# Attention threshold by a parametric relu on ScalarE, q and k loaded into both partition halves, score and output banks shared, whole jobs throughout

## The chip, the cores and the metric

The kernel runs on one core of one Trainium2 chip. The metric is the time of one execution on the device in microseconds (us). TensorE (PE) multiplies, VectorE (DVE) and ScalarE (ACT) work on tiles, GpSimd (POOL) works on tiles in SBUF only, and SyncE (SP) issues the DMAs. Weight loads of TensorE are listed as an engine of their own (PEld).

## The reference

Two stages: an attention that keeps only scores within tau of the row's maximum, and an RWKV channel-mixing layer (called FFN below) over the heads put side by side.

```
q, k, v: (8 batches, 8 heads, 576, 64);  w_k: 512x1024, w_v: 1024x512, w_r: 512x512
scores = 0.125 * q @ k^T                                  # 576 x 576 per head
scores = where(scores >= max(scores) - tau, scores, -1e9) # row by row, tau = 0.02
attn   = exp(scores - max(scores)) / (sum + 1e-9)
x      = (attn @ v), heads side by side                   # 8 x 576 x 512
x_prev = x shifted by one position along the sequence
xk = mu_k*x + (1-mu_k)*x_prev;  xr = mu_r*x + (1-mu_r)*x_prev
out = sigmoid(xr @ w_r) * (relu(xk @ w_k)**2 @ w_v)
```

## The kernel before

**Jobs.** Two heads of a batch make a job; four jobs make a batch, 32 jobs in all. The 576 query rows of a head go as four units of 128 rows ("P" units, both heads, eight score matmuls into two score tiles) and one unit for the last 64 rows of both heads together ("T" unit, eight matmuls, one score tile). So a job has nine softmax passes over a tile of 128x576. Batch 0 alone is cut into eight half jobs (rows 0 to 255, then the rest), so that its first FFN chunk can begin early.

**A softmax pass.** Scores lie in a pair of PSUM banks (tag `s`, two pairs). DVE takes the negated row maximum (L605); ACT makes the threshold column from it (L613) and the exponential of the scores into SBUF (L621); DVE reads scores and exponentials, zeroes what lies under the threshold and sums the rest (L629); DVE inverts the sum (L639, L640), POOL multiplies by it (L654), DVE transposes 32x32 blocks in place (L671, L675). `PV` (L705) multiplies by v: per job 288 small matmuls in one stretch with one weight load each, into four single banks (tag `w`, four banks, shared with the FFN), which ACT copies into `xT` and `xE` (L719, L726).

**Operands.** Matmuls of q and k run in a rounded format, so each is split into a rounded high part and a low rest, stacked on the two partition halves. One DMA each brings q and k; ACT scales q (L429) and rounds both (L469), POOL subtracts (L477), and twelve DMAs move the parts within SBUF to the halves where the matmul wants them (`st<-hiq` and the like). The first job does without (L543).

**FFN.** A chunk is 256 positions: ACT, DVE and POOL make the mixed inputs (L791 to L821), TensorE runs 96 matmuls of 256 columns (L843), 24 of 512 (L885) and 48 of 512 (L907), ACT, POOL and DVE finish (L851 to L913). There are 18 chunks; a batch gives two once its jobs are done, and every fourth batch a third. The 20 weight pieces are prepared in the first stretch, with four DVE passes each (L372 to L403).

**What sets the order.** The order of every engine's instructions is fixed when the program is built: `Plan` lists all steps with a cost and a key, plays them through and issues them in the order of that play. `NUDGE` shifts keys per kind of step. Engines then run their own instructions in this order and wait for each other.

Of the kernel before, what the change touches and what calls it, by code (L numbers as in the profile page):

```python
# [7 lines left out]
F32 = mybir.dt.float32  # L8
# [6 lines left out]

W_MIN = 2.0 ** (0x38 * 2 - 127)
# [24 lines left out]
class Step:  # L41
    __slots__ = (
        "eng", "occ", "lat", "fn", "key", "deps", "succ", "allocs", "idx", "missing", "ready",
        "start", "end", "kb", "soft", "att", "kind",
# [3 lines left out]
class Plan:  # L48
# [3 lines left out]
    HOP, LATE, FROM, AHEAD = 0.05, 0.2, 200.0, 1000.0  # L52
    SOFT = {"DVE": 0.15, "ACT": 0.15}
    NUDGE = {
# [7 lines left out]
    }  # L62

# [12 lines left out]
    def add(self, eng, occ, fn, reads=(), writes=(), key=0.0, lat=None, kb=0, wait=0.0, kind=None):  # L76
        s = Step()
        s.soft = self.SOFT.get(eng, 0.0) if self.soft else 0.0
        s.att = eng == "PE" and key < -500
        if s.att:  # L80
            key += 1000 - self.AHEAD
        s.eng, s.occ, s.fn, s.kb, s.kind = eng, occ, fn, kb, kind
        s.key = key + self.NUDGE.get(kind, 0.0)
# [40 lines left out]
    def order(self, loose=()):  # L124
# [23 lines left out]
        pipe = 0.0  # L148
        out = []
# [22 lines left out]
        while len(out) < total:  # L172
            best = None
            for e, cand in open_.items():
                f = free[e]
                pick = None
                for i in cand:
                    s = steps[i]
                    t = when(s)
                    if t is None:  # L180
                        continue
                    t = max(t, f)
                    k = (t + s.soft, s.key, i, t)
                    if pick is None or k < pick:
                        pick = k
# [8 lines left out]
            free[e] = t + s.occ  # L194
# [3 lines left out]
            else:  # L198
                s.end = t + s.lat
# [11 lines left out]
            for j in s.succ:  # L211
# [4 lines left out]
                n.ready = max(n.ready, t + s.occ if same else s.end + self.HOP + late)  # L216
# [13 lines left out]
def tile_threshold_attention_then_rwkv_ffn(  # L230
# [17 lines left out]
    B, NPAIR, _, _ = qk.shape  # L248
# [9 lines left out]
    W = 2 * S  # L258
# [17 lines left out]
    HALF = 1  # L276
    W0, W1, W2, W3, AVK = 0.653, 1.950, 42.500, 5.365, 1.0
    KC, MV, RES = 2, 0.031, 3
    PREP, VB, LB = 8, 1, {"q": 1, "k": 1}
# [8 lines left out]
    def fixed(name, shape, dtype=F32):  # L288
# [17 lines left out]
        lambda: V.tensor_scalar(small.get()[:, 1:2], small.get()[:, 0:1], 0.0, -1.0, op0=ALU.max, op1=ALU.mult),  # L306
        reads=[(small, 0)],
        writes=[(small, 1)],
        key=-100, kind="dve1",
# [112 lines left out]
    def operands(job, key):  # L422
        b, hp = job["b"], job["hp"]

        def scaled(t):
            add(
                "ACT",
                0.67,
                lambda: A.activation(t()[:, 0:S], t()[:, 0:S], AF.Copy, scale=small.get()[:, 2:3]),  # L429
                reads=[(small, 2)],  # L430
                writes=[raw],
                key=key - PREP, kind="act3",
            )

        if job["plain"]:
            raw = job["raw"] = sbuf("st1", [P, W], F32, 3)
            add("DMA", DQ, lambda: SY.dma_start(raw.get(), qk[b, hp]), writes=[raw], key=key - PREP - 5, kb=576, kind="dma3")
            scaled(raw.get)
# [9 lines left out]
        if job["plain"]:  # L448
            return
        hi, lo = job["hi"], job["lo"] = {}, {}  # L450
        st = job["st"] = [(sbuf("st1", [P, W], FR, 3), sbuf("st2", [P, S], FR, 3)) for _ in range(2)]
        up, dn = slice(0, D), slice(D, P)
        for x, o in (("q", 0), ("k", S)):
            raw = lo[x] = sbuf("lo" + x, [P, S], FR, LB[x])
            top = hi[x] = sbuf("hi" + x, [P, S], FR, 1)
            add(
                "DMA",
                DQ,
                lambda raw=raw, o=o: SY.dma_start(raw.get().bitcast(F32), qk[b, hp, :, o : o + S]),
                writes=[raw],  # L460
                key=key - PREP - 5,
                kb=288, kind="dma5",
            )
            if x == "q":
                scaled(lambda raw=raw: raw.get().bitcast(F32))
            add(
                "ACT",
                0.62,
                lambda raw=raw, top=top: A.activation(top.get(), raw.get().bitcast(F32), AF.Copy),  # L469
                reads=[raw],  # L470
                writes=[top],
                key=key - PREP, kind="act4",
            )
            add(
                "POOL",
                1.39,
                lambda raw=raw, top=top: G.tensor_tensor(  # L477
                    raw.get(), raw.get().bitcast(F32), top.get().bitcast(F32), op=ALU.subtract
                ),
                reads=[top],  # L480
                writes=[raw],
# [538 lines left out]
```

## Time and profile before

| | |
|---|---|
| runs timed | median 1134.08 us of 3 (1131.31 to 1139.18) |
| profiled execution | 1133.43 us, span 1131.3 us |
| PE busy | 922.5 us, 82% of the span |
| DVE busy | 841.9 us, 74% |
| ACT busy | 649.1 us, 57% |
| POOL busy | 573.1 us, 51% |
| DMA | 147.83 MB moved, 131 GB/s on average |

The span is the profile's first to last instruction; the execution's own time lies 2.1 us above it. Matmuls overlap, so a busy share of PE counts some time twice, and so do the others where an instruction starts before the last has written back.

### The profile page before, as it was taken

Reading aid. Unit: us, or ns where it says so; the run is one execution under the profiler, and the core shown is the slowest. Engines: PE = TensorE matmul, PEld = TensorE weight load, DVE = VectorE, ACT = ScalarE, POOL = GpSimd, SP = SyncE. Lnnn points to the kernel's source line nnn. Section 1 sums busy time; section 2 is a strip of 40 time slices with the busy share of each in tenths; the row PEclk is TensorE's granted clock in tenths of the full one; section 3 lists DMA queues with packets and bytes.
Section 4 is the critical chain, followed back from the end, with each engine's and each line's share of the span. In section 5 each row is a group of like instructions: output and inputs, shape, how many; then the busy total and the mean of one; then the engine's idle time right before and its main releaser. Section 6 shows DMA issues by size and latency. Waiting matters only on the chain.

```text
span 1131.3 us, 35156 instructions
## 1 busy us (share of the span) xinstructions
PE 922.5 (82%) x14672; PEld 822.8 (73%) x14672; DVE 841.9 (74%) x1657; ACT 649.1 (57%) x1492; POOL 573.1 (51%) x582
## 2 busy tenths in 40 slices
PE   2334677787688898899899889988989898999988
PEld 2324566776578887888788778877878787888877
DVE  5776977788887888798889798978887988821120
ACT  3434663565456675667576657665766675634432
POOL 3444744454445555565555555555555555443431
PEclk9655788799688999999999999999999999999989
DMA  9376657645444445454545445554545454100000
GB/s 305 110 238 181 213 142 204 175 133 145 128 127 127 141 133 145 129 146 127 139 135 146 127 130 143 131 143 117 146 133 138 128 153 116 57 20 19 20 19 19
DMA packets 57581, 147.83 MB, mean 131 GB/s; under 512 B 9680, under 2 KB 9680, under 8 KB 52816
## 3 DMA queue, kind: packets, MB, share of 16 engines
q1 hardware_dynamic: 57424, 145.60, 45.5%
q8 instruction: 116, 1.90, 0.7%
q14 instruction: 41, 0.34, 0.1%
HBM read 74.19 MB, written 9.44 MB: 74 GB/s over the span
## 4 chain that ended last, share of the span: by engine, by line
PE 49%; DVE 24%; issue 12%; ACT 9%; POOL 5%; DMA 1%; SPq 0%; POOLq 0%; ACTq 0%; DVEq 0%
PE w L705 16%; PE s L559 9%; PE w L843 9%; PE w L907 8%; DVE sq L671 6%; PE w L885 6%; DVE sm L605 6%; DVE sq L629 6%; DVE r L800 3%; ACT sq L621 3%; POOL sq L654 2%; PE s L526 1%; ACT k L856 1%; ACT sm L613 1%; DVE sg L913 1%
## 5 line engine op out<-in xcount | busy, mean ns | idle before, releaser
L654 POOL TENSOR_SCALAR sq<-sq,sm 128x576 f32<-128x576 f32 x288 | 227.3, 802 | 235.5 <-DVE sm L640 228.0
L605 DVE TENSOR_REDUCE sm<-s 128x1 f32<-128x576 f32 x288 | 212.5, 751 | 117.1 <-PE s L559 102.3
L705 PE MATMUL w<-sq,v 32*64 32x144 f32 (+2 forms) x10368 | 193.3, 297 | 121.3 <-issue 98.2
L705 PEld LDWEIGHTS w<-sq,v 32*64 32x64 f32 x10368 | 172.3, 146 | 142.3 <-issue 114.2
L629 DVE SCALAR_TENSOR_TENSOR sq<-s,sm,sq 128x576 f32<-128x576 f32 x288 | 226.2, 803 | 24.7 <-ACT sq L621 23.3
L843 PE MATMUL w<-xk,wk 128*128 128x256 f32 x1728 | 226.9, 289 | 8.1 <-ACT xk L813 4.0
L843 PEld LDWEIGHTS w<-xk,wk 128*128 128x128 f32 x1728 | 221.0, 195 | 11.3 <-POOL xk L821 5.0
L907 PE MATMUL w<-wv,k 128*128 128x512 f32 x864 | 214.8, 396 | 0.4 <-ACT xE L726 0.4
L621 ACT ACTIVATE sq<-s,sm 128x576 f32<-128x576 f32 x288 | 208.9, 726 | 0.2
L671 DVE STREAM_TRANSPOSE sq<-sq 128x1152 f32<-128x1152 f32 x128 | 175.4, 1371 | 16.1 <-POOL sq L654 15.9
L907 PEld LDWEIGHTS w<-wv,k 128*128 128x128 f32 x864 | 161.3, 191 | 31.2 <-ACT xE L726 0.7
L559 PE MATMUL s<-st 128*128 128x288 f32 x504 | 125.4, 333 | 56.9 <-DVE sq L629 41.6
L613 ACT ACTIVATE sm<-sm,small 128x1 f32<-128x1 f32 x288 | 83.8, 291 | 151.1 <-DVE sm L605 139.5
L559 PEld LDWEIGHTS s<-st 128*128 128x128 f32 x504 | 89.5, 205 | 84.0 <-issue 58.8
L821 POOL TENSOR_TENSOR xk<-r,xk 128x512 fp32r<-128x512 f32 x72 | 92.4, 1283 | 101.8 <-ACT xk L813 100.7
L866 POOL TENSOR_TENSOR k<-r,k 128x512 fp32r<-128x512 f32 x72 | 93.9, 1305 | 73.1 <-ACT k L856 73.0
L559 PE MATMUL s<-st,st 128*128 128x288 f32 x504 | 117.0, 315 | 0.6 <-issue 0.6
L800 DVE SCALAR_TENSOR_TENSOR r<-r,mu_sb,xT 128x256 f32<-128x256 f32 x128 | 74.3, 620 | 52.5 <-POOL r L791 44.1
L885 PE MATMUL w<-wr,xk 128*128 128x512 f32 x432 | 107.8, 391 | 0.0
L719 ACT ACTIVATE xT<-w 128x128 f32<-128x128 f32 (+1 forms) x144 | 34.5, 288 | 99.7 <-PE w L705 99.7
L559 PEld LDWEIGHTS s<-st,st 128*128 128x128 f32 x504 | 89.2, 207 | 1.1 <-issue 1.1
L885 PEld LDWEIGHTS w<-wr,xk 128*128 128x128 f32 x432 | 78.1, 188 | 13.2
(55 smaller groups left out, 899.1 us busy)
## 6 DMA issues: line engine op xcount, KB each, us to landing
v<-in_v SPq DMA_DIRECT2D x36, 1152.0 KB, 5.1
st<-hiq SPq DMA_DIRECT2D x140, 144.0 KB, 2.5
st<-loq SPq DMA_DIRECT2D x140, 144.0 KB, 2.6
loq<-in_qk SPq DMA_DIRECT2D x35, 288.0 KB, 2.9
lok<-in_qk SPq DMA_DIRECT2D x35, 288.0 KB, 3.0
st<-hik SPq DMA_DIRECT2D x70, 144.0 KB, 2.8
st<-lok SPq DMA_DIRECT2D x70, 144.0 KB, 3.0
out<-sg SPq DMA_DIRECT2D x32, 256.0 KB, 2.3
```

The lines of the kernel that those rows point to most:

```text
L559: PE.matmul(ss[y].get()[:, z, 0:HS], l.get()[:, c * P : (c + 1) * P], r.get()[:, keys(z)], start=(j == 0), stop=(j == 1),)
L605: lambda sv=sv, col=col: V.tensor_reduce(col(0), sv(), axis=AX.XY, op=ALU.max, negate=True),
L613: lambda col=col: A.activation(col(1), col(0), AF.Identity, bias=small.get()[:, 1:2], scale=-1.0),
L621: lambda st=st, pv=pv, col=col: A.activation(pv(), st(), AF.Exp, bias=col(0)),
L629: lambda st=st, pv=pv, col=col: V.scalar_tensor_tensor(pv(), st(), col(1), pv(), op0=ALU.is_ge, op1=ALU.mult, accum_out=col(2)),
L654: lambda y=y: G.tensor_scalar(part(y), part(y), sm.get()[:, 3, y : y + 1], 0.0, op0=ALU.mult, op1=ALU.add),
L671: V.transpose(t, t)
L705: PE.matmul(os[a].get()[hs, 0:n], vt.get()[rows, j, hs], sq.get()[rows, j, h, lo:hi], start=(j == 0), stop=(j == NB - 1),)
L800: V.scalar_tensor_tensor(d.get()[:, y, o : o + n], diff.get()[:, y, o : o + n], mu_sb.get()[:, j, hc + y : hc + y + 1], prv[:, hc + y], op ...
L843: PE.matmul(h.get()[:, f], l, r, start=(ct == 0 and i == 0), stop=(ct == NCT - 1 and i == 2))
L885: PE.matmul(z.get(), l, r, start=(ct == 0 and i == 0), stop=(ct == NCT - 1 and i == 2))
L907: PE.matmul(vps.get(), l, r, start=(ft == 0 and i == 0), stop=(ft == NFT - 1 and i == 2))
```

## The change

The mask is made on ACT. The bias column is the negated maximum plus tau; a parametric relu with slope 1e30 leaves scores above the threshold as they are (shifted by tau) and throws those below far down, straight out of PSUM into SBUF (L640); a second pass in place takes the exponential with a bias of minus tau and sums the row (L648). DVE keeps the maximum and a one-column addition (L632) in place of the mask. The host lays each head of q and k out twice, once per partition half, and a DMA per head brings each (L463, L471); ACT rounds q with its scale (L498) and k (L480), DVE makes the low part of q in one pass (L508), POOL subtracts on one half of k (L488); no move within SBUF is left. `PV` writes two pairs of tag `s`, which has three pairs now; `w` has two banks for the FFN alone. The output copies are two per kind and job (L743, L750). `PV` is issued in three pieces, the second and third not before a set distance from the one ahead. Batch 0 has whole jobs like the others, and the first job has no path of its own. `Plan` also has a term for the fetch of PE's instructions in blocks of 256, and new tables of numbers.

```diff
-    SOFT = {"DVE": 0.15, "ACT": 0.15}
+    SOFT = {"DVE": 0, "ACT": 0}
...
+    CHUNK, FETCH = 256, 3.55
...
+            if s.ni:
+                more = self.CHUNK - code % self.CHUNK
+                code += s.ni
+                while more <= s.ni:
+                    at = t + stall + s.occ * more / s.ni
+                    stall += max(0.0, turned + self.FETCH - at)
...
+        for h in range(2):
+            rk, rq = sbuf("rk", [P, S], F32, RB), sbuf("rq", [P, S], F32, RB)
...
+                lambda rk=rk, both=both: A.activation(both.get(), rk.get(), AF.Copy),
...
+                    both.get()[D:P], rk.get()[D:P], both.get()[D:P].bitcast(F32), op=ALU.subtract
...
+                lambda rq=rq, top=top, low=low: V.scalar_tensor_tensor(
...
-            for h in range(2):
-                sl = slice(h * D, (h + 1) * D)
-                moves = [(st[h][0], up, top), (st[h][0], dn, raw)]
...
-        ss = {y: psum("s", [P, 2, 512], 2) for y in ys}
+        ss = {y: psum("s", [P, 2, 512], 3) for y in ys}
...
-                lambda col=col: A.activation(col(1), col(0), AF.Identity, bias=small.get()[:, 1:2], scale=-1.0),
+                "DVE",
+                0.1,
+                lambda col=col: V.tensor_scalar(col(1), col(0), small.get()[:, 1:2], None, op0=ALU.add),
...
-                lambda st=st, pv=pv, col=col: A.activation(pv(), st(), AF.Exp, bias=col(0)),
+                lambda st=st, pv=pv, col=col: A.activation(pv(), st(), AF.Prelu, bias=col(1), alpha=STEEP),
...
-                lambda st=st, pv=pv, col=col: V.scalar_tensor_tensor(
-                    pv(), st(), col(1), pv(), op0=ALU.is_ge, op1=ALU.mult, accum_out=col(2)
...
+                lambda y=y, col=col: A.activation(part(y), part(y), AF.Exp, bias=small.get()[:, 3:4], accum_out=col(2)),
...
-        os = [psum("w", [P, 512], 4) for _ in range(4)]
+        os = [psum("s", [P, 2, 512], 3) for _ in range(2)]
...
+                after=(prev, GAP * ni) if k else None,
...
-            h = psum("w", [P, 2, CH], 4)
+            h = psum("w", [P, 2, CH], NF)
...
-    halved = {j: ([0, 1], [2, "T", 3]) for j in range(HALF)}
-    PLAIN = 1
...
-    plan.order(loose=("w", "r"))
+    plan.order(loose=("w", "r", "s", "sm"))
```

Two places show how the order moves. The first is PE in the middle of the program: before, the last three rows of a job's `PV` (`w_67..` are its output banks), the score matmuls that follow (`s_69..`) and the FFN (L843).

```order
L705 MATMUL w_6742<-sq_6218,v_6476 64x144
L705 MATMUL w_6744<-sq_6218,v_6476 64x144
L705 MATMUL w_6746<-sq_6218,v_6476 64x144
L559 MATMUL s_6906<-st_2_6554 128x288 x2
L559 MATMUL s_6906<-st_2_6554,st_1_6570 128x288 x2
L559 MATMUL s_6916<-st_1_6279 128x288 x2
L559 MATMUL s_6916<-st_1_6279,st_0_6288 128x288 x2
L843 MATMUL w_6925<-xk_6375,wk_0_585 128x256 x3
```

The same kind of place in the change: the end of the second piece of a job's `PV`, six FFN matmuls (L932, the old L907), and the start of the third piece; `s_7081` and `s_7084` are the pairs that the job's output fills.

```order
L717 MATMUL s_7084<-sq_6616,v_6844 64x144 x2
L717 MATMUL s_7081<-sq_6616,v_6844 64x144 x2
L717 MATMUL s_7084<-sq_6616,v_6844 64x144 x2
L932 MATMUL w_7146<-wv_0_1336,k_0_6656 128x512 x3
L932 MATMUL w_7146<-wv_0_1428,k_0_6656 128x512 x3
L717 MATMUL s_7081<-sq_6616,v_6844 64x144 x2
L717 MATMUL s_7084<-sq_6616,v_6844 64x144 x2
```

Before, all 144 rows of a job's `PV` stand in one stretch with nothing between; now FFN or score matmuls stand between its three pieces. After the last `PV` of the program, four FFN chunks and half of an L907 stage follow before; three chunks and a little over half of such a stage follow now.

The second place is ACT in the middle of the program, before: threshold columns (`sm`), exponentials out of the score tiles (`sq<-s`) and the FFN's relu, square and copy.

```order
L613 ACTIVATE sm_6818<-sm_6818,small 128x1
L621 ACTIVATE sq_6647<-s_6906,sm_6818 128x18x32
L613 ACTIVATE sm_6935<-sm_6935,small 128x1
L621 ACTIVATE sq_6647<-s_6916,sm_6935 128x18x32
L851 ACTIVATE r_6968<-w_6925 128x512
L852 ACTIVATE r_6968<-r_6968 128x512
```

In the change, with relus out of the score tiles (L640), exponentials in place with their sums (L648), and the rounding of q and k (L498, L480):

```order
L640 ACTIVATE sq_6207<-s_6447,sm_6388 128x18x32
L838 ACTIVATE xk_6256<-r_6491 128x512
L648 ACTIVATE sq_6207,sm_6388<-sq_6207,small 128x18x32
L498 ACTIVATE qa_6523<-rq_6142,small 128x576
L480 ACTIVATE kc_6529<-rk_6160 128x576
L640 ACTIVATE sq_6207<-s_6471,sm_6514 128x36x16
L640 ACTIVATE sq_6207<-s_6462,sm_6479 128x18x32
L648 ACTIVATE sq_6207,sm_6514<-sq_6207,small 128x36x16
```

The one-column step is gone from ACT, and each pass over a score tile stands twice, once out of PSUM and once in SBUF.

## Rows read from the trace of the kernel before

**Rows 1.** Windows: engines' busy time (instructions), clock, DMA, in three stretches.

```profile
0.00:200.00 200.00, 104.23 (x2351) 91.33 (x2352) 150.88 (x268) 95.70 (x222) 97.39 (x89) 0.75 0.67 198
200.00:998.00 798.00, 695.89 (x11563) 623.24 (x11561) 669.50 (x1330) 505.12 (x1189) 430.18 (x451) 0.96 0.48 133
998.00:1131.30 133.30, 122.43 (x760) 108.19 (x760) 21.53 (x61) 48.31 (x82) 45.55 (x43) 0.97 0.06 19
```

**Rows 2.** Windows of line L605 alone, the row maximum, one per softmax pass.

```profile
0.00:200.00 200.00, 27.08 (x37) 0.75 0.67 198
200.00:998.00 798.00, 185.41 (x252) 0.96 0.48 133
```

**Rows 3.** The chain that ended last, around one `PV` in the middle.

```profile
571.25 3.68 PE w L705 x218
574.93 0.98 issue
575.92 1.45 PE w L705 x68
```

**Rows 4.** Waits (engine, line, what for): totals over 0 to 200 us.

```profile
PEld w L705 <- issue: 56.1, 16, 9.4
```

**Rows 5.** Waits, totals over 200 to 998 us.

```profile
PEld w L705 <- issue: 56.8, 51, 2.6
...
PEld s L559 <- issue: 41.3, 43, 3.7
```

**Rows 6.** Timeline of PE: starts of score matmuls, and of what follows eight.

```profile
561.16 0.43 PE L559 MATMUL s<-st 128*128 128x288 f32 x2
...
562.23 4.11 PE L843 MATMUL w<-xk,wk 128*128 128x256 f32 x33
```

**Rows 7.** The chain that ended last, in the stretch after the last `PV`.

```profile
998.67 1.31 PE w L705 x64
...
1036.13 10.88 PE w L843 x89
1047.00 5.48 PE w L885 x24
...
1065.48 10.89 PE w L843 x89
...
1115.70 10.89 PE w L907 x48
```

**Rows 8.** Groups by line and shape: count, busy us, mean ns of one, idle before.

```profile
L629 DVE SCALAR_TENSOR_TENSOR sq<-s,sm,sq 128x576 f32<-128x576 f32 x288 | 226.2, 803 | 24.7 <-ACT sq L621 23.3
L621 ACT ACTIVATE sq<-s,sm 128x576 f32<-128x576 f32 x288 | 208.9, 726 | 0.2
...
L613 ACT ACTIVATE sm<-sm,small 128x1 f32<-128x1 f32 x288 | 83.8, 291 | 151.1 <-DVE sm L605 139.5 <-DVE sm L639 8.8
...
L429 ACT ACTIVATE loq<-loq,small 128x576 f32<-128x576 f32 x35 | 26.9, 767 | 0.0
...
L469 ACT ACTIVATE hiq<-loq 128x576 fp32r<-128x576 f32 x35 | 23.6, 675 | 0.2
...
L629 DVE DVE_READ_ACCUMULATOR sq<-s,sm,sq 128x1 f32 x288 | 23.5, 82 | 0.0
...
L386 DVE TENSOR_SCALAR xT<-xT 128x512 uint32<-128x512 uint32 x20 | 12.8, 646 | 0.1
...
L639 DVE TENSOR_SCALAR sm<-sm 128x1 f32<-128x1 f32 x32 | 4.7, 146 | 0.5
```

**Rows 9.** Timeline of ACT: an exponential and the next instruction's start.

```profile
563.28 0.72 ACT L621 ACTIVATE sq<-s,sm 128x576 f32<-128x576 f32 x1
563.91 0.28 ACT L613 ACTIVATE sm<-sm,small 128x1 f32<-128x1 f32 x1
```

**Rows 10.** Timeline: scores of one tile begin on PE, and its mask on DVE.

```profile
549.00 0.67 PE L559 MATMUL s<-st 128*128 128x288 f32 x2
...
552.61 0.82 DVE L629 SCALAR_TENSOR_TENSOR sq<-s,sm,sq 128x576 f32<-128x576 f32 x1
```

More of the change, by code (lines that the diff above doesn't have):

```diff
@@ L14 @@
 U32 = mybir.dt.uint32
+STEEP = 1e30
+TAU = 110.0
 W_MIN = 2.0 ** (0x38 * 2 - 127)
@@ L198, in order @@
             else:
-                s.end = t + s.lat
+                s.end = t + s.lat + stall
             for b in s.allocs:
@@ L215, in order @@
                 late = self.LATE if n.att and t > self.FROM else 0.0
-                n.ready = max(n.ready, t + s.occ if same else s.end + self.HOP + late)
+                n.ready = max(n.ready, t + s.occ + stall if same else s.end + self.HOP + late)
                 if n.missing == 0:
@@ L423, in operands @@
         b, hp = job["b"], job["hp"]
-        def scaled(t):
+        job["st"] = []
+        for h in range(2):
+            rk, rq = sbuf("rk", [P, S], F32, RB), sbuf("rq", [P, S], F32, RB)
+            add(
+                "DMA",
+                DQ,
+                lambda rq=rq, h=h: SY.dma_start(rq.get(), qk[b, hp, h, :, :S]),
+                writes=[rq],
+                key=key - PREP - 5,
+                kb=288, kind="dma5",
+            )
+            add(
+                "DMA",
+                DQ,
+                lambda rk=rk, h=h: SY.dma_start(rk.get(), qk[b, hp, h, :, S:]),
+                writes=[rk],
+                key=key - PREP - 5,
+                kb=288, kind="dma3",
+            )
+            top, low, both = (sbuf(t, [P, S], FR, 3) for t in ("qa", "qb", "kc"))
@@ L432, in scaled @@
+            add(
+                "ACT",
+                0.7,
+                lambda rq=rq, top=top: A.activation(
+                    top.get(), rq.get(), AF.Copy, scale=small.get()[:, 2:3]
+                ),
+                reads=[rq, (small, 2)],
+                writes=[top],
                 key=key - PREP, kind="act3",
             )
[L435 to L438, printed above, removed]
+            add(
+                "DVE",
+                0.8,
+                lambda rq=rq, top=top, low=low: V.scalar_tensor_tensor(
+                    low.get(),
+                    rq.get(),
+                    small.get()[:, 2:3],
+                    top.get().bitcast(F32),
+                    op0=ALU.mult,
+                    op1=ALU.subtract,
+                ),
+                reads=[rq, top, (small, 2)],
+                writes=[low],
+                key=key - PREP, kind="dve7b",
+            )
@@ L439, in operands @@
+            job["st"].append((top, low, both))
         vt = job["v"] = sbuf("v", [P, NB, P], F32, VB)
@@ L447, in operands @@
         )
[L448 to L481, printed above, removed]
-                key=key - PREP, kind="pool2",
-            )
-            for h in range(2):
-                sl = slice(h * D, (h + 1) * D)
-                moves = [(st[h][0], up, top), (st[h][0], dn, raw)]
-                if x == "q":
-                    moves += [(st[h][1], dn, top), (st[h][1], up, raw)]
-                for dst, rows, src in moves:
-                    fn = (lambda dst=dst, rows=rows, src=src, sl=sl, o=o: SY.dma_start(
-                        dst.get()[rows, o : o + S].bitcast(F32), src.get()[sl].bitcast(F32)
-                    ))
-                    add("DMA", DQ, fn, reads=[src], writes=[(dst, (rows.start, x))], key=key - PREP, kb=144, kind="dma6")
     def scores(unit, ss, key):
@@ L936, in tile_threshold_attention_then_rwkv_ffn @@
     for b in range(B):
-        for part, order in enumerate(halved.get(b, ([0, "T", 1, 2, 3],))):
-            for hp in range(NPAIR):
-                job = dict(ji=len(jobs), b=b, hp=hp, first=n, sq=None, plain=len(jobs) < PLAIN, units=[])
-                job.update(tail="T" in order)
-                for u in order:
-                    kind = "T" if u == "T" else "P"
-                    job["units"].append(dict(job=job, kind=kind, c=u, n=n))
-                    n += 1 if kind == "T" else 2
-                jobs.append(job)
+        for hp in range(NPAIR):
+            job = dict(ji=len(jobs), b=b, hp=hp, first=n, sq=None, units=[])
+            for u in ORDER:
+                kind = "T" if u == "T" else "P"
+                job["units"].append(dict(job=job, kind=kind, c=u, n=n))
+                n += 1 if kind == "T" else 2
+            jobs.append(job)
     wlist = [
@@ L969, in tile_threshold_attention_then_rwkv_ffn @@
             key = unit["n"] - 30.0
-            for g in sorted({u["c"] // 2 for u in job["units"] if u["kind"] == "P"}):
+            for g in range(2):
                 if g == 1:
```

180 lines of the change are left out of this document (98 added, 82 removed), and 22 rows, old and new, of the table NUDGE.

## Prediction

> **What bounds the kernel now.** I read the windows first, cut where the work changes: up to 200 us batch 0 runs and the weights are prepared, up to 998 us the other 28 jobs run with FFN chunks between them, and after the last `PV` the FFN runs alone [rows 1]. The row maxima confirm the cut: 37 passes in the first stretch, one more than the 36 of four jobs, and 252, which is 28 times nine, in the second [rows 2]. So a job costs 200/4 = 50 us at first and 798/28 = 28.5 us later. The end costs 133.3 us.
>
> In the middle stretch DVE is busy 84% and ACT 63%, but PE is nearest to its limit, and its busy time hides how near, since matmuls overlap. I count PE by starts instead. `PV` runs 218 matmuls in 3.68 us when nothing stops it, so 288 take 4.86 us [rows 3]. Eight score matmuls take 562.23 - 561.16 = 1.07 us, and five such groups 5.35 us [rows 6]. An FFN chunk is 89 matmuls in 10.88 us, so 11.7 us for 96, and 5.48 and 10.89 us for its other stages: 28.1 us [rows 7]. In the order one chunk falls in the first stretch and 4.2 after the last `PV`, which leaves 12.8 of 18 for 28 jobs, 12.9 us per job. PE then works 4.86 + 5.35 + 12.9 = 23.1 us of 28.5. Of the missing 5.4 us, (56.8 + 41.3)/28 = 3.5 us are waits put down to "issue" at `PV` and the scores behind it [rows 5]: no semaphore was outstanding, and the stop comes in the middle of the small matmuls [rows 3]. I read it as instructions that arrive slower than 32x64 matmuls use them up. About 1.9 us are waits for other engines.
>
> In the first stretch both things are worse: "issue" costs 56.1 us at `PV` alone, up to 9.4 us at once [rows 4], while the DMA engines are busy 67% and the clock stands at 0.75 on average [rows 1]; and DVE, with the weights to prepare, is busy 150.9 of 200 us.
>
> **The change part by part.**
>
> *Mask off DVE.* Each of 288 passes loses 0.803 + 0.082 us on DVE and gains a one-column addition; the nearest row is a one-column operation of 0.146 us [rows 8]. Per job DVE falls from 669.5/28 = 23.9 us by 9 x 0.74 = 6.7. The low part of q, two passes a job, is a two-input pass of 128x576 such as the mask was, 0.80 us each [rows 8], so DVE is at 18.8 us plus a little for FFN that moves in. It stops being near a bound.
>
> *Two passes on ACT.* A job loses nine threshold columns of 0.291 us (2.6 us) and keeps nine passes out of PSUM, relu in place of exponential, at 0.726 us [rows 8]. It gains nine exponentials in SBUF with a sum. The pass itself I take at the same 0.726 us; the sum's read-out isn't in this trace, and I bound it by DVE's read-out of 0.082 us and by ACT's own one-column instruction of 0.291 us, and take 0.2, nearer to the latter because it is the same engine. That is 9 x 0.93 = 8.3 us. Rounding q and k goes from 0.767 + 2 x 0.675 = 2.1 to 2 x 0.767 + 2 x 0.675 = 2.9 us [rows 8]. The output copies fall from eight to four wider ones; I count nothing for it. With two more chunks in this stretch (below), at 48.3/4.2 = 11.5 us of ACT each [rows 1], ACT goes from 505.1/28 = 18.0 to 18.0 - 2.6 + 8.3 + 0.8 + 0.8 = 25.3 us of busy time per job. Some of this is overlap: the next instruction began 0.63 us after an exponential of 0.72 us [rows 9], 0.09 us less for each of some 45 instructions. So ACT is truly taken 21 to 25 us.
>
> The row says that ACT passes over the scores in 0.73 us where DVE needs 0.89 [rows 8]. The Trainium skill speaks against the move: "ScalarE: Activation LUTs", Rules for kernel authors, wants relu and the like on VectorE rather than ScalarE. For 32-bit scores out of PSUM the row decides against that advice as to the price of a pass, but as to the load it stands: by it ACT would be the new limit, which is the first rival.
>
> *`PV` in three pieces.* Six FFN matmuls (0.7 to 1.4 us) stand between pieces in the order, so that PE has work while instructions arrive. At best the 3.5 us per job go; at worst nothing goes. I take all of it: the stall seen is 0.98 us behind 218 matmuls [rows 3], and 96 matmuls now run before a break.
>
> *One chunk from the end to the middle, one from the start.* After the last `PV` there are now 3.2 chunks. The end costs 29.4 us less, which is one chunk's period there, 1065.48 - 1036.13 [rows 7], and 0.7 us more for three matmuls of an L907 stage: 133.3 - 28.7 = 104.6 us. The first stretch now holds no chunk until batch 0's scores are through. So the middle carries 14.8 chunks, 14.9 us of PE per job.
>
> *Middle, summed.* PE works 4.86 + 5.35 + 14.9 = 25.1 us. I keep the 1.9 us of other waits, and add 0.5 because ACT's free time shrinks from ten to three or four us: 27.5 us per job, 770 us for 28.
>
> *First stretch.* DVE's 150.9 us fall by 37 x 0.74 = 27.4; eight low parts add 6.4; 24 of the 80 weight passes come after batch 0 in the order, at 0.646 us [rows 8] 15.5 us. That leaves 114 us. At the old share of 75% it takes 152 us, at the middle's 84% 136 us [rows 1]. PE's side gives the same: no chunk (28 us), and 1152 `PV` matmuls in place of 2304, which takes up to half of the 56 us of "issue" [rows 4]: 200 - 28 - 28 = 144 us. I take 145, and 125 to 170 as its ends.
>
> *DMA.* Twelve moves within SBUF per job go; inputs grow from 576 to 1152 KB. By these sizes a job moves about 2.3 in place of 2.9 MB, and the engines were busy 48% in the middle [rows 1]. I cost it at nothing; the cover is that jobs' inputs are ordered ahead.
>
> *Sum.* 145 + 770 + 105 = 1020 us of span, and 2.1 us outside it as in the profiled execution before: **1022 us**. That execution, 1133.4 us, agrees with the median of 1134.1 within 0.1%. A difference under 1% is no more than a measurement of this kernel can tell from none.
>
> **The rivals.**
>
> *ACT takes over as the bound.* The read-out at its upper bound makes 26.1 us of ACT; if little of it overlaps and ACT waits as PE does (2.4 us), a job takes 28.5 us, 798 us in the middle, 1050 us in all. For it: ACT's queue is fixed, relus and exponentials of one tile depend on each other, and the FFN's own passes stand between. Against it: the 0.63 us steps [rows 9].
>
> *The instructions still arrive too slowly.* If the pieces hide nothing, a job takes 27.5 + 3.5 = 31.0 us and the whole 145 + 868 + 105 + 2 = 1120 us; half hidden, 1071 us. For it: the total of instructions per `PV` is unchanged, and the breaks are short. Against it: long stretches ran before they stopped [rows 3].
>
> *Slower than before: scores starved of banks.* `PV` now fills two of the three pairs, and only one is left for scores until ACT has copied the output. A tile was held from 549.00 to 553.43, 4.4 us [rows 10]. Let `PV` and its copies take 8 us and a tile be held h: eight us serve 8/h passes, and the other 9 - 8/h run on three pairs at h/3 each, together 5.3 + 3h us a job. At 4.4 that is 18.5 and no bound. It would decide from h = 7.4 (27.5 us). A tile's hold ends with the relu now, earlier than with the mask, but a relu that queues behind the FFN on a fuller ACT could hold it 9 us: 32.3 us a job, 904 us, 1156 us in all. The page gives little for this, as DVE and PE would have to leave ACT that far behind.
>
> *Better than forecast.* If nearly all waits go, a job takes 25.1 us and the first stretch 130: 940 us.
>
> **How the numbers follow.** Forecast 0.52 (975 to 1045), ACT bound 0.20 (1045 to 1075), instructions 0.15 (1060 to 1120), bank pairs 0.05, better 0.08. The range 970 to 1100 leaves out most of the last two and the top of the instructions case, less than 0.2 in all. Faster by over 1%, below 1122.7 us, is nearly everything but the bank pairs: 0.91; within 1% 0.04; slower 0.05.
>
> **What would show it.** The 37th row maximum near 145 us instead of 200; row maxima 27.5/9 = 3.1 us apart on average in the middle; "issue" waits at `PV` in the middle well under 1 us per job; relus and exponentials near 0.73 us, with a read-out of 0.1 to 0.3; ACT busy about nine tenths there; 105 us from the last `PV` on. The prediction is wrong if relu or exponential in place take over 1 us, if PE waits for the relu (L640) to free tiles, or if the first stretch still takes 180 us because DMA traffic keeps PE's instructions waiting.

## The result, and the profile after

The changed kernel takes 1007.8 us (median of four runs, 1007.6 to 1010.6), the kernel before 1133.6 us in the runs beside it: a ratio of 0.889, 95% interval 0.885 to 0.893. The profiled execution's span is 1005.8 us, and its 37th row maximum begins at 126 us.

Busy time of each engine over the span, from the page of after. Time in which two instructions of an engine overlap counts once in it, not twice as stated above: the 1660 instructions of ACT add up to 939 us and keep it busy for 795.

```profile
PE 900.2 (90%) x13520; PEld 790.3 (79%) x13520; DVE 705.8 (70%) x1434; ACT 794.9 (79%) x1660; POOL 588.6 (59%) x576
```

Windows of after, cut near the 37th row maximum, at 200 us and at the end of the last `PV` (length, then busy us and count of PE, PEld, DVE, ACT and POOL, then the granted clock, the DMA share and GB/s); they answer to [rows 1]:

```profile
0.00:128.00 128.00, 60.76 (x1036) 50.97 (x1036) 110.15 (x209) 90.94 (x193) 67.86 (x65) 0.74 0.49 177
128.00:200.00 72.00, 60.31 (x1002) 52.19 (x1001) 61.36 (x117) 58.71 (x125) 51.45 (x47) 0.82 0.21 73
200.00:905.00 705.00, 686.94 (x10952) 605.63 (x10953) 516.59 (x1057) 609.22 (x1285) 434.86 (x432) 1.00 0.29 96
905.00:1005.80 100.80, 92.24 (x552) 81.48 (x534) 17.66 (x52) 36.06 (x59) 34.43 (x34) 0.97 0.07 22
```

From 200 us to the last `PV`, PE is now busy 97%, ACT 86% and DVE 73%. Per job (27.8 us) that is 24.0 us of ACT (predicted 25.3) and 20.4 of DVE (predicted 18.8 and a little).

Groups of after by line (count, busy us, mean ns of one, idle before), which answer to [rows 8]:

```profile
L648 ACT ACTIVATE sq<-sq,small 128x576 f32<-128x576 f32 x288 | 222.9, 777 | 2.0
...
L640 ACT ACTIVATE sq<-s,sm 128x576 f32<-128x576 f32 x288 | 206.4, 737 | 59.2 <-DVE sm L632 55.5 <-DVE sm L656 3.1 <-PE w L868 0.2
...
L508 DVE SCALAR_TENSOR_TENSOR qb<-rq,small,qa 128x576 fp32r<-128x576 f32 x64 | 61.1, 957 | 3.7 <-ACT qa L498 3.5
L648 ACT ACTIVATION_READ_ACCUMULATOR sq<-sq,small 128x1 f32 x288 | 57.0, 198 | 0.0
L632 DVE TENSOR_SCALAR sm<-sm,small 128x1 f32<-128x1 f32 x288 | 56.4, 198 | 2.2
```

Waits of after from 128 to 905 us (us in total, times, longest), which answer to [rows 5]. PEld is the weight load, PE the matmul:

```profile
PEld s L578 <- ACT sq L640: 16.0, 22, 3.3
PEld s L717 <- issue: 15.2, 44, 1.4
...
PE s L578 <- ACT sq L640: 10.1, 12, 3.1
...
PEld s L578 <- issue: 7.3, 34, 0.5
...
PE s L717 <- issue: 1.7, 3, 1.0
```

The two "issue" waits of [rows 5], 98 us together, are 22.5 us now. But they are idle times of the weight load, and PE can be busy in them or wait for something else. PE's own waits before, from 200 to 998 us:

```profile
PE w L705 <- issue: 44.7, 33, 2.3
PE s L559 <- DVE sq L629: 32.5, 26, 2.5
...
PE s L559 <- issue: 4.4, 4, 1.6
```

So PE itself stood 49 us for "issue" in that stretch, not 98, and stands 2 us now. Of the 41.3 us at the scores, the traces set side by side give 22 in which PE waited for a tile that the mask still held, and 11 in which it was busy. All of PE's waits for other engines were 53 us there and are 28 now.

PE's wait for a free score tile has changed its releaser: for the P units it was 41.6 us in the whole run on DVE's mask (L629) before, and is 37.6 us on ACT's relu (L640) now. The timeline of PE in after, around one `PV` (start, duration, instruction, idle before):

```profile
510.05 1.77 PE L717 MATMUL s<-sq,v 32*64 32x144 f32 x96 [0.26 <-DVE sm L657]
...
512.38 0.86 PE L932 MATMUL w<-wv,k 128*128 128x512 f32 x3
513.17 1.78 PE L717 MATMUL s<-sq,v 32*64 32x144 f32 x96
514.88 1.65 PE L932 MATMUL w<-wv,k 128*128 128x512 f32 x6
516.46 1.78 PE L717 MATMUL s<-sq,v 32*64 32x144 f32 x96
```

Against [rows 3], none of the three pieces is broken, and nothing is idle between them and the FFN.

### The profile page after: what moved, and what is told of

It reads as the page before. It is cut to its first block, busy times and chain, and to the rows that moved or that the text cites. A ratio compares the mean times of both kernels' runs of the same rounds, so it can differ in the third digit from the quotient of the medians.

```text
span 1005.8 us, 32052 instructions
## 1 busy us (share of the span) xinstructions
PE 900.2 (90%) x13520; PEld 790.3 (79%) x13520; DVE 705.8 (70%) x1434; ACT 794.9 (79%) x1660; POOL 588.6 (59%) x576
## 4 chain that ended last, share of the span: by engine, by line
PE 43%; DVE 9%; ACT 4%; POOL 3%; issue 2%; ACTq 0%; DVEq 0%; POOLq 0%
PE w L868 13%; PE s L717 8%; PE w L932 7%; PE w L910 7%; PE s L578 6%; DVE r L825 3%; DVE sm L624 2%; DVE sq L688 2%; PE s L562 2%; POOL sq L671 1%; POOL xk L846 1%; ACT sq L640 1%; ACT sq L648 1%; ACT L648 1%; DVE sm L656 1%
## 5 line engine op out<-in xcount | busy, mean ns | idle before, releaser
L671 POOL TENSOR_SCALAR sq<-sq,sm 128x576 f32<-128x576 f32 x288 | 239.4, 843 | 162.4 <-DVE sm L657 90.6
L640 ACT ACTIVATE sq<-s,sm 128x576 f32<-128x576 f32 x288 | 206.4, 737 | 59.2 <-DVE sm L632 55.5
L648 ACT ACTIVATE sq<-sq,small 128x576 f32<-128x576 f32 x288 | 222.9, 777 | 2.0
L932 PE MATMUL w<-wv,k 128*128 128x512 f32 x864 | 215.2, 394 | 0.0
L717 PE MATMUL s<-sq,v 32*64 32x144 f32 x9216 | 177.8, 292 | 19.2 <-issue 8.4
L717 PEld LDWEIGHTS s<-sq,v 32*64 32x64 f32 x9216 | 151.0, 133 | 44.2 <-issue 23.8
L932 PEld LDWEIGHTS w<-wv,k 128*128 128x128 f32 x864 | 157.8, 188 | 32.5 <-issue 3.6
L578 PE MATMUL s<-kc,qa 128*128 128x288 f32 x512 | 128.4, 334 | 50.3 <-ACT sq L640 37.6
L578 PEld LDWEIGHTS s<-kc,qa 128*128 128x128 f32 x512 | 88.7, 204 | 78.0 <-ACT sq L640 35.2
L488 POOL TENSOR_TENSOR kc<-rk,kc 64x576 fp32r<-64x576 f32 x64 | 96.8, 1517 | 82.0 <-issue 60.8
L578 PE MATMUL s<-kc,qb 128*128 128x288 f32 x512 | 117.7, 314 | 0.0
L578 PEld LDWEIGHTS s<-kc,qb 128*128 128x128 f32 x512 | 89.5, 205 | 1.2 <-issue 1.2
L838 ACT ACTIVATE xk<-r 128x512 fp32r<-128x512 f32 x72 | 45.2, 628 | 54.6 <-DVE r L825 54.3
```

The lines of the kernel that those rows point to most:

```text
L578: PE.matmul(ss[y].get()[:, z, 0:HS], l.get()[:, c * P : (c + 1) * P], r.get()[:, keys(z)], start=(j == 0), stop=(j == 1),)
L640: lambda st=st, pv=pv, col=col: A.activation(pv(), st(), AF.Prelu, bias=col(1), alpha=STEEP),
L648: lambda y=y, col=col: A.activation(part(y), part(y), AF.Exp, bias=small.get()[:, 3:4], accum_out=col(2)),
L671: lambda y=y: G.tensor_scalar(part(y), part(y), sm.get()[:, 3, y : y + 1], 0.0, op0=ALU.mult, op1=ALU.add),
L717: PE.matmul(os[a // 2].get()[hs, a % 2, 0:NX], vt.get()[rows, j, hs], sq.get()[rows, j, h], start=(j == 0), stop=(j == NB - 1),)
L932: PE.matmul(vps.get(), l, r, start=(ft == 0 and i == 0), stop=(ft == NFT - 1 and i == 2))
```

## The experiments

Each ratio is to the kernel before on the same chip, whose median lay between 1133.6 and 1140.9 us. So "us of before" below is the difference of ratios times 1133.6, which leaves the chip out; by the intervals it is good to some 5 to 8 us. The last three columns count the row maxima of each trace: when the 37th of 288 begins, how long nine take on average from the 73rd to the 285th (one job), and what remains behind the last.

| kernel | us | ratio (95%) | against after, us of before | 37th | per job | behind the last |
|---|---|---|---|---|---|---|
| before | 1133.6 | 1 | +126 | 200 | 28.4 | 145 |
| after | 1007.8 | 0.889 (0.885 to 0.893) | 0 | 126 | 27.3 | 120 |
| e1_one_piece | 1047.8 | 0.920 (0.917 to 0.924) | +36 | 135 | 28.8 | 129 |
| e2_mask_dve | 1136.5 | 0.996 (0.994 to 0.998) | +121 | 128 | 30.2 | 116 |
| e3_act_load | 1046.1 | 0.919 (0.916 to 0.922) | +34 | 129 | 28.6 | 121 |
| e3b_dve_load | 1247.0 | 1.096 (1.092 to 1.099) | +234 | 155 | 35.2 | 120 |
| e3c_dve_load1 | 1097.0 | 0.962 (0.956 to 0.967) | +82 | 139 | 30.2 | 120 |
| e4_less_pe | 988.9 | 0.869 (0.866 to 0.872) | -23 | 122 | 26.9 | 120 |
| e5_banks | 1126.1 | 0.987 (0.981 to 0.994) | +111 | 119 | 30.1 | 165 |
| e6_before_whole | 1192.6 | 1.046 (1.040 to 1.052) | (before +52) | 133 | 30.6 | 176 |
| e7_no_tables | 1110.4 | 0.973 (0.969 to 0.978) | +96 | 136 | 30.7 | 116 |
| e8_dma_moves | 1060.7 | 0.931 (0.925 to 0.936) | +47 | 145 | 28.8 | 119 |
| e9_square_dve | 1049.6 | 0.920 (0.915 to 0.925) | +35 | 128 | 28.8 | 130 |
| e10_no_eps | 994.4 | 0.872 (0.868 to 0.876) | -20 | 124 | 27.0 | 120 |

**e1_one_piece.** `PV` in one stretch.

```diff
-KC, MV, RES, NF, SW, GAP = 3,
+KC, MV, RES, NF, SW, GAP = 1,
```

> The output matmuls of a job (PV) in one stretch again instead of three pieces, everything else as in the change (the order is played through anew). Theory A: the pieces with FFN or score matmuls between them hide the late arrival of PE's instructions. Then the issue waits at PV between 200 and 905 us, 15 us in the change, come back towards the 57 us of before, up to 3.5 us per job: 1045 to 1100 us. Rival: the waits went because a job's DMA traffic fell (97 MB in place of 148 MB in all); then the time stays within 1% of 1008 us and the issue waits stay under 25 us.

The timeline of PE in this run shows the last 172 matmuls of one `PV`, and the waits from 136 to 940 us the sum:

```profile
499.73 0.68 PE L717 MATMUL s<-sq,v 32*64 32x144 f32 x26
501.60 2.27 PE L717 MATMUL s<-sq,v 32*64 32x144 f32 x128 [1.18 <-issue]
505.32 0.70 PE L717 MATMUL s<-sq,v 32*64 32x144 f32 x18 [1.46 <-issue]
```

```profile
PEld s L717 <- issue: 50.2, 40, 2.0
...
PE s L717 <- issue: 39.5, 35, 1.8
...
PEld s L578 <- issue: 7.3, 30, 1.4
```

The stops are back (39.5 us of PE, where after has 1.7), and with them 36 us. The order was played anew, so that not all of the 36 need be the stops. That they are late instructions can be read from where they fall. Counted in PE's own order, with weight loads and semaphore instructions, the 36 stops of over 0.6 us at this run's `PV` all lie at the same place of a grid of 256 instructions, to within one; so do 42 of 47 before. Between the two stops shown there are 128 matmuls with their 128 weight loads. The stops at the scores behind `PV` (41.3 us in [rows 5]) stay away without pieces: for the most part they were waits for the mask, as PE's own rows show, and no business of the pieces.

**e3_act_load, e3b_dve_load, e3c_dve_load1.** The very order of the change, with work that nobody needs on one engine in each softmax pass: a copy of 128x256 behind each relu on ACT, or two passes (e3b) or one pass (e3c) of 128x256 behind the column addition on DVE.

```diff
+                    A.activation(junk.get()[:, 0:256], junk.get()[:, 0:256], AF.Copy),
...
+                        V.scalar_tensor_tensor(junk.get(), junk.get(), 1.0, junk.get(), op0=ALU.mult, op1=ALU.mult)
```

> A copy of 128x256 on a tile that nobody else uses behind each of the 288 relus on ScalarE, in the very order of the change: about 0.30 us each by start to start, 2.7 us per job. Theory A: the middle is bound by PE and ScalarE has 3 to 5 us free per job; then the time grows by 5 to 20 us, most of it before 200 us where PE waits for the relu: 1013 to 1028 us. Rival: ScalarE is the bound after the change (it is busy 86% there); then 28 jobs pay 2.7 us each and the time is 1075 to 1090 us.

> Two passes of 128x256 with two inputs on a tile that nobody else uses behind each one-column addition on VectorE, in the very order of the change: about 0.66 us per softmax pass and 6 us per job, nearly what the mask took there before. Theory A: the middle is bound by PE, so the load costs the first stretch (38 passes by 0.66, 25 us) and little after it: 1030 to 1050 us. Rival: taking the mask off VectorE is what made the middle faster; then 28 jobs pay 2 us or more each on top and the time is 1085 us or more.

> The load on VectorE again, with one pass of 128x256 in place of two, 0.605 us each in the run before, so 5.4 us per job, less than the 6.7 us that the mask took; the order is that of the change. Theory B, after the first runs: in the middle PE and ScalarE limit each other and VectorE has some 9 us free per job; the load costs the first stretch up to 38 x 0.6 = 23 us and the middle under 1 us per job: 1030 to 1055 us. Rival: the middle needs VectorE's relief; 2 us or more per job, 1085 us or more.

The added groups, in e3_act_load and in e3c_dve_load1:

```profile
L644 ACT ACTIVATE junk<-junk 128x256 f32<-128x256 f32 x288 | 120.0, 417 | 0.0
```

```profile
L637 DVE SCALAR_TENSOR_TENSOR junk<-junk 128x256 f32<-128x256 f32 x288 | 162.1, 563 | 0.0
```

On ACT 120 us cost 34, 0.3 us for each, between the two expectations. On DVE e3b put on 349 us, nearly twice what was meant, so e3c is the fair test: 162 us cost 82, 0.5 for each. Part of these durations is overlap: ACT's busy time rose by 79 us and DVE's by 131, and by that measure the prices are 0.4 and 0.6. Either way half or more of the load on an engine that was busy 73% shows in the time, as the rival of e3c had it. Part of DVE's price is not DVE's alone: the added pass took 404 to 421 ns where no GpSimd pass ran beside it, and its mean is 563 (last section). The waits of e3c, whole run, show the path: DVE is late with the relu's bias, and PE with the tiles that the relu frees.

```profile
ACT sq L648 <- DVE sm L635: 105.6, 92, 5.1
...
PE s L580 <- ACT sq L648: 59.1, 47, 8.7
```

In after these two are 55.5 and 37.6 us.

**e4_less_pe.** The second of the two score products is left out in the P units, 512 of 13520 matmuls, in the order of the change.

```diff
-                    for z in range(2):
+                    for z in range(2 - 2 * j):
```

> The second product of the scores (the low part of q with k) is left out for the units of 128 rows, 16 of a job's 40 score matmuls, in the very order of the change; all else runs. PE loses 16 x 0.134 = 2.1 us per job. Theory A (the middle is bound by PE): 25 to 28 jobs gain 1.5 to 2.1 us each, 945 to 972 us. Rival (ScalarE or the chain through it is the bound): under 10 us gained, 998 to 1008 us.

By [rows 6] these are 512 x 0.134 = 69 us of PE; 23 came back, 0.3 for each, and 989 us lies between the two expectations. By PE's busy time, which fell by 43 us, it is 0.5, so that PE's price can't be told from the other two. In the waits of this run PE's wait for the relu grew from 37.6 to

```profile
PE s L578 <- ACT sq L640: 51.6, 55, 9.7
```

**e2_mask_dve.** The threshold goes back to DVE; the rest of the change stays.

```diff
-                lambda st=st, pv=pv, col=col: A.activation(pv(), st(), AF.Prelu, bias=col(1), alpha=STEEP),
+                lambda st=st, pv=pv, col=col: A.activation(pv(), st(), AF.Exp, bias=col(0)),
...
+                lambda st=st, pv=pv, col=col: V.scalar_tensor_tensor(
+                    pv(), st(), col(1), pv(), op0=ALU.is_ge, op1=ALU.mult, accum_out=col(2)
```

> Only the threshold goes back: one exponential out of PSUM on ScalarE, mask and sum on VectorE; all other parts of the change stay, and the order is played through anew with the same tables. ScalarE loses about 8 us per job, VectorE gains 6 to 7 (18.4 to about 25). Theory B: VectorE is then the engine with the least room, in the first stretch above all (38 passes by 0.74, 28 us), and the time is 1040 to 1080 us, so that the relu itself is worth 3 to 7 of the 11%. Rival: the relu is worth nothing and the other parts carry the gain: 1000 to 1015 us. Second rival: the relu carries nearly all of it: 1110 us or more.

The page of this run:

```profile
PE 948.2 (84%) x13520; PEld 823.1 (73%) x13520; DVE 921.6 (81%) x2010; ACT 601.6 (53%) x1086; POOL 586.1 (52%) x576
```

All but nothing is left of the gain. Yet DVE's 216 us more and ACT's 193 us less make only 0.6 x 216 - 0.4 x 193 = 52 us by the loads above; the other 70 may belong to an order that was not made for this mix (e7). Some of them are TensorE's clock, which was granted at 0.900 on average in this run and at 0.948 in after (next section).

**e5_banks.** Two score pairs as before, and `PV` into four single banks with eight copies.

```diff
-        ss = {y: psum("s", [P, 2, 512], 3) for y in ys}
+        ss = {y: psum("s", [P, 2, 512], 2) for y in ys}
...
-        os = [psum("s", [P, 2, 512], 3) for _ in range(2)]
+        os = [psum("w", [P, 512], NF) for _ in range(4)]
```

> The banks go back: two pairs for scores, PV into four single banks shared with the FFN, and eight output copies per job instead of four; all else as in the change. Theory B: with two pairs the scores wait longer for the relu, and ScalarE pays 0.8 us more per job: 1015 to 1060 us. Rival: sharing the third pair is what lets PV be cut into pieces at all, and without it most of the middle's gain goes: 1075 us or more. Second rival: the pairs that PV fills starve the scores in the change, and the time falls below 1000 us.

In the order of PE 16 of 32 jobs have `PV` in three pieces here (27 in after), 7 in two, and 9 in one stretch, as this one:

```profile
508.32 2.98 PE L717 MATMUL w<-sq,v 32*64 32x144 f32 x175 [0.78 <-DVE sg L938]
512.87 1.98 PE L717 MATMUL w<-sq,v 32*64 32x144 f32 x107 [1.57 <-issue]
```

The order also left about one and a half more chunks behind the last row maximum (165 against 120 us). So banks, pieces and order can't be taken apart by this run.

**e6_before_whole.** The kernel before without half jobs and without the first job's own path.

```diff
-    HALF = 1
+    HALF = 0
-    PLAIN = 1
+    PLAIN = 0
```

> The kernel before with whole jobs in batch 0 and no path of its own for the first job; its tables and all else stay. Theory: the eight half jobs run twice the output matmuls of four whole ones, and PE stood 56 us for instructions there; half of that goes and the first FFN chunk comes later: 1095 to 1125 us. Rival: the half jobs pay for themselves by the early FFN chunk, and the time is 1130 to 1160 us.

The 37th row maximum begins at 133 instead of 200 us, and the whole is 5% slower, which neither expectation had: FFN and weights were moved behind it (176 us remain behind the last row maximum), in an order whose tables were made for half jobs.

**e7_no_tables.**

```diff
-    NUDGE = {
-        "act1": -59.5, "act10": 67.0, "act11": -222.0, "act12": -115.0, "act13": 59.5, "act14": -52.5, "act15": 165.0,
...
+    NUDGE = {}
+    FIRST, UNTIL = {}, 60.0
```

> The changed kernel with NUDGE and FIRST emptied, so that keys alone order the play; every instruction is the same, only their order on the engines differs. It tells how much of the gain hangs on an order that was tuned for just this mix of work, and so how far the runs that take one part back (relu, banks, half jobs) suffer from an order that was not tuned for them. Theory: engines wait for each other in fixed queues, and a poor order costs as much as a single part of the change, 50 to 120 us: 1060 to 1130 us, issue waits not grown by more than 20 us, waits between PE, DVE and ACT grown instead. Rival: the work alone sets the time and the tables are trimming, under 30 us: 1005 to 1038 us.

The same instructions in another order cost 96 us. The waits of this run, whole span, have what was 17.2 + 37.6 us of PE in after (the scores stand at L562 here) as

```profile
PE s L562 <- ACT sq L624: 92.6, 41, 15.0
```

The theory holds. It also means that a part taken back in an order not made for it (e1, e2, e5, e6, e8, e9) may cost more than the part is worth.

**e8_dma_moves.**

```diff
+            for t in (top, low, both):
+                for o in (0, D):
+                    add(
+                        "DMA",
+                        DQ,
+                        lambda rq=rq, t=t, o=o: SY.dma_start(t.get()[o : o + D].bitcast(F32), rq.get()[o : o + D]),
```

> The changed kernel with twelve moves of 144 KB within SBUF per job put back ahead of the operands' own writes, whose data overwrite them (55 MB more traffic in all, as much as the change took away). Theory, as in the prediction: the moves are hidden, since the jobs' inputs are ordered ahead; at most 10 us: 1008 to 1018 us. Rival: the moves lie between a job's inputs and its first scores and on SP's queue, and their traffic slows PE's instructions (the first stretch had its longest stops where the DMA engines were busiest): 30 us or more, 1038 us or above, with issue waits up by 15 us and the 37th row maximum past 140 us.

The theory fell. Waits of PE in this run, 0 to 145 us:

```profile
PE s L589 <- DMA kc<-rq: 19.7, 1, 19.7
PE s L589 <- DMA wv<-in_w_v: 17.6, 1, 17.6
PE s L728 <- issue: 13.8, 2, 12.9
```

The first is a wait for the added moves: POOL's subtraction, which makes `kc`, itself waits for one of them here,

```profile
POOL kc L499 <- DMA qa<-rq: 17.8, 1, 17.8
```

and PE begins at 19.7 us, where after begins at 10.3. The second is no wait for a transfer, though the profile names one: the scores don't read `wv`, and the `kc` that they read came at 49.1 us from POOL. POOL and ACT had been at work on steps that stand ahead of it in this order, with no wait for a transfer from 32 us on. The third stop lies from 75 to 88 us, where the DMA engines were busy 25% of the time, so that their load is not shown to be its cause. So of the 19 us by which the 37th row maximum is later, 9 are shown to be the moves.

From 200 us on the chain that ended last holds four moves,

```profile
327.59 8.03 DMA qa<-rq
...
413.94 3.75 DMA qb<-rq
...
563.29 4.19 DMA qb<-rq
...
710.32 4.67 DMA qb<-rq
```

20.6 us together, where the chain of after holds none. So the moves are on the path there too; how much of the 1.5 us per job is theirs and how much the order's stays open.

**e9_square_dve.** The FFN's square goes from ACT to DVE.

```diff
-            add("ACT", 0.53, lambda r=r: A.activation(r.get(), r.get(), AF.Square), writes=[r], key=key - 1, kind="act12")
+            add("DVE", 0.6, lambda r=r: V.tensor_tensor(r.get(), r.get(), r.get(), op=ALU.mult), writes=[r], key=key - 1, kind="act12")
```

> The changed kernel with the FFN's square taken from ACT to DVE (one instruction of 128x512 per half stage; it is replayed, so the order may shift). ACT loses 45 to 55 us of its 795, DVE gains 50 to 70 on its 706. Theory from the loads put on: ACT's microseconds cost 0.3 to 0.4 and DVE's 0.5, so that the move is worth nothing or costs up to 20 us: 1005 to 1028 us. Rival: ACT, at 86% in the middle, is the engine nearest its limit after PE and any relief pays: 985 to 1000 us.

Neither: 35 us slower. The square takes longer on DVE than the 630 ns it took on ACT, in this run's groups

```profile
L877 DVE TENSOR_TENSOR r<-r 128x512 f32<-128x512 f32 x72 | 61.2, 850 | 39.4 <-ACT r L876 38.9
```

and by the loads above it costs 0.5 x 61 - 0.3 x 45 = 17 us; the order of PE differs too, from about its 1420th of 13520 matmuls on.

**e10_no_eps.**

```diff
-            V.tensor_scalar(sm.get()[:, 2, ysl], sm.get()[:, 2, ysl], 1e-9, None, op0=ALU.add)
```

> The changed kernel without the addition of 1e-9 to the row sums ahead of the reciprocal: 160 small DVE instructions go, 34 us of DVE's busy time; a row's largest term is about 1, so that the sum in 32 bits is unchanged by it. The order of PE, ACT, POOL and SP is the same. Theory: DVE, though busy 70%, still costs about half a microsecond per microsecond (one load of 174 us cost 89), and the instruction lies between the exponential's sum and the multiplication by its inverse: 34 us less gives 12 to 20 us: 988 to 996 us. Rival: taking load away finds other waits in its place and gives less than 5 us: 1003 to 1010 us.

994.4 us, the fastest but for e4, which leaves a product out: 13 us below after, 20 by the ratios. The intervals of the two ratios do not meet. So 38.6 us of small DVE instructions were worth 0.35 to 0.5 us for each microsecond, as e3c has it, and PE's wait for the relu, whole run, fell from 37.6 to

```profile
PE s L578 <- ACT sq L640: 24.3, 21, 4.5
```

## Why the prediction was right, and where its steps were not

The forecast, 1022 us, is 1.4% above the result, and the sign, the range and the likeliest case hold. By its terms: 145 + 770 + 105 was predicted, 126 + 779 + 101 came. That the total is so near is partly luck: an early first stretch and a late middle offset each other, and within the middle two errors did.

**First stretch: right in kind, off in size.** The 37th row maximum came at 126 us, near the lower end. Of the 56.1 us of "issue" at `PV` in [rows 4], 8.7 are left in the first 128 us of after, where the prediction let half go; and DVE, whose work was sized well (110 us against 114), runs at 86%, not 75%. The prediction did carry a chunk from here to the middle, and e6 shows why that matters: this marker moves when FFN is moved behind it, and whole jobs put into the kernel before cost 5%.

**Middle: the sum holds, by two errors.** 27.8 us per job against 27.5. Late instructions were the right suspect, and the pieces the right cure (e1), but the term was twice too large: "(56.8 + 41.3)/28 = 3.5 us" takes the idle time of the weight load for PE's. By PE's own rows it was 49/28 = 1.8 us per job, and it went almost wholly (0.1 left). Taking the pieces back costs 1.5 us per job (28.8 against 27.3). The stops at the scores were mostly PE waiting for the mask. The other error has the opposite sign: PE's waits for other engines, 53/28 = 1.9 us per job as the prediction had it, were said to grow to 2.4 and fell to 1.0. Together 3.6 us per job of waiting became 1.1, a gain of 2.6 where 3.0 was booked. What is left between PE's counted work and the job, 1.8 us before and 1.6 now, was read as waits too; the trace shows no wait of PE in it, and part of it is the lower clock below.

**A term that was left out: TensorE's clock.** Its two levels are 1.2 and 2.4 GHz, and the granted clock is 0.921 of the higher on average before and 0.948 in after. So PE stood at the lower level for about 2 x 0.079 x 1131 = 179 us before and 2 x 0.052 x 1006 = 105 us now, and was busy in 110 and in 63 us of it, counted in the traces. The same 96 `PV` matmuls at either level, both in after:

```profile
135.23 3.19 PE L717 MATMUL s<-sq,v 32*64 32x144 f32 x96
...
194.40 1.78 PE L717 MATMUL s<-sq,v 32*64 32x144 f32 x96
```

At that ratio about 20 of the 126 us (an estimate) are work of PE that is done at the higher level now. In the runs with long waits it goes the other way: PE was busy 140 us at the lower level in e2 and 125 in e7, so that some 34 and 27 of their 121 and 96 us are the clock's, by the same estimate. A wait of PE can cost twice, once as itself and once as slower matmuls behind it.

**"It stops being near a bound" failed.** DVE was written off after its load fell to about 19 us of 27.5. In e3c each microsecond put on it costs 0.5 to 0.6, more than on ACT (0.3 to 0.4); what PE gives back (0.3 to 0.5) lies between. The prediction counted PE's work per job, added a fixed 2.4 us of waits, and took the rest as free. In fact PE, ACT and DVE each run a fixed order and wait for each other's small steps (row maximum, bias column, relu, free tile), so that all three share the bound. DVE's load was itself short, 20.4 us per job against 18.8: the mask with its read-out, credited at 0.885 us, held DVE only 0.75 from start to next start (216 us in 288 passes), and the low part of q took 0.15 us more than was said.

**ACT as the new bound: neither fell nor held.** The sizes were close (relu 737 ns for 726, exponential 777 for 726, read-out 198 for 200), and ACT is busy 86% where nine tenths were said. That PE waits for the relu was named as a sign of being wrong. The wait is there: 38 us of the first 126 at the P and T units together, and small after that, 15.5 us from 128 to 905 us. The rule that relu belongs on VectorE (the Trainium skill, "ScalarE: Activation LUTs", Rules for kernel authors) did not pay in this kernel: e2, with the threshold on DVE as a mask, is 12% slower than after, though some of that may be order.

**"DMA: I cost it at nothing" failed.** With the moves put back, PE's first matmul comes 9 us later, behind a wait for them, and four moves of 20.6 us stand on the chain in the middle, where after has none. The rest of the 47 us that e8 lost may be its order. That its first stretch took 145 us, the number that the prediction had without any credit for DMA, is chance as far as the runs show: order and a stop of 12.9 us are in it.

**The starved banks** didn't come; e5 points the other way, since with two pairs for scores and four banks for `PV` nearly the whole gain is gone, for whichever of its reasons.

**The gain isn't a sum of parts.** Taken back one at a time, relu, banks, tables, moves and pieces cost 121, 111, 96, 47 and 36 us, 411 of a gain of 126. At least part of each figure is the order, and how much belongs to the relu alone is not settled.

## What to carry to other kernels

Before calling an engine free because it is busy 70%, put a known load on it in the same order and read the price: here DVE cost 0.5 to 0.6 us per microsecond, and leaving out a small instruction between two steps of the chain was worth 13 to 20 us. Before booking an engine's idle time as a loss, read the waits of the engine that does the work: a weight load that idles while matmuls run, or while they wait for a tile, is not TensorE losing time to its instructions. Where the order is fixed when the program is built, a part undone in an order made for the whole tells the part and the order together; loads and omissions that leave the order as it is tell more. A marker in the middle of a run shows a gain only if the work behind it is looked at too.

## What the runs showed of the hardware

**A DVE pass in SBUF has a long tail, beside GpSimd only.** The low part of q (L508) takes 810 ns in the median, as the mask did that read one input from PSUM, but 957 on average and 2.04 us at most, where the mask stayed within 767 to 820 ns. Of its 64 passes, 18 ran with no GpSimd pass beside them, and none of these took over 819 ns; the 31 that met a two-input pass of GpSimd took 1069 on average. The timelines of DVE and of POOL in after show a long one beside two-input passes of POOL, and one of 0.88 us beside a one-input pass (L671):

```profile
208.18 0.88 DVE L508 SCALAR_TENSOR_TENSOR qb<-rq,small,qa 128x576 fp32r<-128x576 f32 x1
211.16 2.04 DVE L508 SCALAR_TENSOR_TENSOR qb<-rq,small,qa 128x576 fp32r<-128x576 f32 x1
```

```profile
207.71 1.98 POOL L671 TENSOR_SCALAR sq<-sq,sm 128x576 f32<-128x576 f32 x2 [1.29 <-DVE sm L657]
209.77 2.81 POOL L488 TENSOR_TENSOR kc<-rk,kc 64x576 fp32r<-64x576 f32 x2
212.66 1.70 POOL L846 TENSOR_TENSOR xk<-r,xk 128x512 fp32r<-128x512 f32 x1
```

The Trainium skill ("SBUF — State Buffer", Who interferes with whom) says that a DVE instruction with two SBUF inputs contends with GpSimd instructions that read SBUF; the tails agree, here and in e3c (404 to 1641 ns, median 416) and e9 (644 to 1927, median 692). This is why the prediction's 0.80 us for this pass, read from the mask, was too small by 0.15, and part of why load on DVE is dear. Two inputs are not needed for a tail: the one-input weight pass L405 took up to 418 ns alone and up to 1644 beside GpSimd. The row maximum, whose input is in PSUM, has none (712 to 760 ns).

**Small instructions aren't small.** ACT's read-out of a sum takes 198 ns where DVE's takes 82 [rows 8], and the one-column addition on DVE 198 ns where the nearest row said 146.

**Stops in a stretch of short matmuls come on a grid.** In e1 all 36 stops of over 0.6 us at `PV` lie 256 TensorE instructions apart, or a multiple of that, to within one; from 136 us on they last up to 1.8 us. Pieces of 96 matmuls with other work between them leave 1.7 us of such stops from 128 to 905 us in after.

**The clock is low in a wait and just behind it.** In e8 PE did one matmul between 75 and 88 us, was granted 0.50 in that window and still 0.50 from 88 to 91 us, when it was busy again; from 94 to 97 us it was granted 1.00.
